# Loading the first x tile in one piece, splitting the rest of W1, and an uneven last chunk, in a kernel that TensorE bounds

## The chip, the cores and the metric

The kernel runs on one core of a Trainium2 chip. The metric is device time in microseconds (us) of that core. All runs compared here are of the state "fast". The profile shows one execution; its span (first to last instruction) is 1.3 to 1.4 us shorter than the device time of the same execution.

TensorE is "PE" in the profile (its weight loads are "PEld"), VectorE is DVE, ScalarE is ACT, GpSimd is POOL, and SP (SPq) is the engine whose queue issues most transfers. A label such as L624 is a line of the kernel that the trace belongs to; the same matmuls are L620 in the changed kernel.

## The reference

For x of 2048 rows and 640 features, all in bf16:

```python
g = sigmoid((x * gate_w).sum(-1))                 # one gate per row
Bu = x @ B_bar.T                                  # complex
h[t] = Lam_bar * h[t-1] + Bu[t]                   # a linear recurrence over the rows
a = 2 * Re(h @ C.T) + x * Dskip
b = gelu(x @ w1 + b1) @ w2 + b2                   # 640 -> 1728 -> 640
out = g * a + (1 - g) * b
```

The front of the program, which the change is about, is the first product `x @ w1` for the first 512 rows. It needs x with features on partitions (xT), and W1.

## The kernel before

The front loads W1 in five slabs of 128 features. For slabs 0 and 1 of x, a plain load brings rows onto partitions and TensorE transposes them; slabs 2 to 4 come by a DMA transpose. The rest of W1's columns (1024 to 1727) is one load. Here are the parts that matter, with cuts marked by `...`:

```python
xnat(0, 0)                                   # x slab 0: 128 x 4 x 128, pieces of 256 B
for h in range(2):                           # W1 slab 0, two halves, pieces of 1024 B
    load(f"w1_0{h}", "sp", ...)
xnat(1, 1.2)                                 # x slab 1, pieces of 256 B
w1load(1, "sp", 1.3)                         # W1 slab 1, pieces of 2048 B
w1load(2, "sp", 2)
xtrans(0, range(KN, KD), 3, 1.8)             # x slabs 2 to 4 by DMA transpose
w1load(3, "sp", 4)
w1load(4, "sp", 5)
load("w1_r", "sp", "l_w1r", W1sb[:, :, FW:F], ...)          # rest of W1, pieces of 1408 B
# then the DMA transposes of B
...
# five small parameter rows, issued on ScalarE's queue; the last is the tail of b1
load("b1b", "act", "l_b1b", rows[RT:RT + 1, :]..., ["b1b"], prio=-96, dur=0.4)
...
for n in (512, 512, 512, 512, 512, 256):     # TensorE warms up on constants
    t = nc.tensor.matmul(PS[5][:, 0:n], one.broadcast_to([128, 128]), ...)
...                                          # per slab: 4 transposes, one copy of 128 x 512; then a fill matmul
op("cols", "pe", 0.3, list(ROWS) + ["b1b", "ident"], [("bank", 7)], f_cols, prio=9.5)   # rows -> columns
...
seq = [(k, jf) for k in range(KD) for jf in range(NW)]      # 40 matmuls: 5 slabs x 8 banks
...
# end: the last chunk's output in two halves of 320 columns, each combined and stored on its own
```

A small list scheduler orders each engine's work when the program is built. "cols" turns the parameter rows into columns with one transpose on TensorE, between the ninth and the tenth of the 40 matmuls.

Of the kernel before, what the change touches and what calls it, by code (L numbers as in the profile page):

```python
# [184 lines left out]
def bass_gated_mix__ssm_conv_s5__dense_activation_gelu__prompt_kernel(  # L185
# [40 lines left out]
    with ExitStack() as es:  # L226
# [76 lines left out]
        def inc(eng, ins):  # L303
            return E.inc(eng, ins, eng + "_s")
# [46 lines left out]

        KN = 2

        def xnat(k, prio):
            load(f"xna{k}", "sp", f"l_xna{k}", xn[0][:, :, k * 128:(k + 1) * 128],
                 x2[0:512, k * 128:(k + 1) * 128].rearrange("(c p) d -> p c d", p=128), [("xna", k)], prio, dur=0.45, lat=2.0)

        xnat(0, 0)
        for h in range(2):
            fs = slice(h * FW // 2, (h + 1) * FW // 2)  # L360
            load(f"w1_0{h}", "sp", f"l_w10{h}", W1sb[:, 0, fs], B_w1[0:128, fs], [("w1", 0, h)], 0.1 + h, dur=0.45, lat=2.0)
        xnat(1, 1.2)
        w1load(1, "sp", 1.3)
        w1load(2, "sp", 2)
        xtrans(0, range(KN, KD), 3, 1.8)
        w1load(3, "sp", 4)
        w1load(4, "sp", 5)
        load("w1_r", "sp", "l_w1r", W1sb[:, :, FW:F], B_w1[:, FW:F].rearrange("(k p) f -> p k f", p=128), [("w1", "r")], prio=20, lat=5.0)

        ROWS = {"lre": (0, A_Lambda_re), "lim": (KP, A_Lambda_im), "ldt": (2 * KP, A_log_dt), "b1a": (3 * KP, B_b1[0:nmain])}  # L370
        RT = 3 * KP + NF - 1
# [27 lines left out]

        def f_warm():  # L400
            t = None
            for n in (512, 512, 512, 512, 512, 256):
                t = nc.tensor.matmul(PS[5][:, 0:n], one.broadcast_to([128, 128]), one.broadcast_to([128, n]), start=True, stop=True)
            return inc("pe", t)

        op("warm", "pe", 2.5, (), [("bank", 5)], f_warm, prio=-1000)

        for k in range(KN):
            bank = 7 - k
            pt = PS[bank][:, :].bitcast(BF16)[:, 0:512]  # L410

            def f_xt(k=k, pt=pt):
                t = None
                for c in range(4):
                    t = nc.tensor.transpose(pt[:, c * 128:(c + 1) * 128], xn[0][:, c, k * 128:(k + 1) * 128], ident[:, :])
                return inc("pe", t)

            op(f"xt{k}", "pe", 0.44, [("xna", k), "ident"], [("bank", bank)], f_xt, prio=(-990, 4.5)[k])

            def f_xc(k=k, pt=pt):  # L420
                return inc("dve", nc.vector.tensor_copy(out=xT[0][:, k, :], in_=pt))

            op(f"xc{k}", "dve", 0.42, [("bank", bank)], [("xT", 0, k)], f_xc, prio=-2000 + k)

        def f_fill():
            return inc("pe", nc.tensor.matmul(PS[5][:, :], one.broadcast_to([128, 128]), one.broadcast_to([128, 512]), start=True, stop=True))

        op("fill", "pe", 0.4, (), [("bank", 5)], f_fill, prio=-980)

        XT = {q: [("xT", q, k) for k in range(KD)] for q in range(NQ)}  # L430

        psC = PS[7][:, :].bitcast(BF16)[:, 0:128]

# [135 lines left out]
        for ci, src in enumerate((A_B_re, A_B_im)):  # L569
# [1 line left out]
        xtrans(1, range(KD), 32, 3.4)  # L571
        load("gwb", "sp", "l_gwb", gwb[:, :], gate_w.partition_broadcast(128), ["gwb"], prio=32.2)
        load("xnb", "sp", "l_xnb", xn[0][:, :, KN * 128:D], x2[0:512, KN * 128:D].rearrange("(c p) d -> p c d", p=128),
             [("xn", 0, 0), ("xn", 0, 1)], 32.4, dur=1.0, lat=6.0, reads=[("xna", 0), ("xna", 1)])
        load("w2a", "sp", "l_w2a", W2sb[:, 0:NF - 1, :], B_w2[0:nmain, :].rearrange("(j p) d -> p j d", p=128), ["w2a"], prio=33, lat=8.0)
        load("w2b", "sp", "l_w2b", W2sb[0:FL, NF - 1, :], B_w2[nmain:F, :], ["w2b"], prio=34, lat=4.0)
        load("w2c", "sp", "l_w2c", W2sb[64:64 + FL, NF - 1, :], B_w2[nmain:F, :], ["w2c"], prio=34.2, lat=4.0)
# [39 lines left out]
        def m1_first():  # L617
            seq = [(k, jf) for k in range(KD) for jf in range(NW)]
            seq.remove((0, NW - 1))
            seq.insert(seq.index((1, NW - 1)), (0, NW - 1))  # L620
            for k, jf in seq:

                def f_mm(jf=jf, k=k):
                    return inc("pe", nc.tensor.matmul(PS[jf][:, :], W1sb[:, k, jf * 128:(jf + 1) * 128], xT[0][:, k, :],  # L624
                                                      start=(k == 0), stop=(k == KD - 1)))

                op(f"m1_0_{jf}_{k}", "pe", d_mm(512), [("xT", 0, k), ("w1", k) if k else ("w1", 0, jf // (NW // 2))], [("bank", jf)] ,
                   f_mm, prio=pe_prio())
            for jf in range(NW):
                ctr["bank"] += 1  # L630

                def f_ge(jf=jf):
                    return inc("act", nc.scalar.activation(Gl[0][:, jf, :], PS[jf][:, :], ACT.Gelu_apprx_tanh, bias=b1col[:, jf:jf + 1]))

                op(f"ge_0_{jf}", "act", d_act(512), [("bank", jf), "b1col"], [("gl", 0, jf)], f_ge, prio=10)

        def m1(q, j0=0):
            for jf in range(j0, NF - 1):
                bank = next_bank()

                def f_mm(jf=jf, bank=bank):
                    t = None
                    for k in range(KD):
                        t = nc.tensor.matmul(PS[bank][:, :], W1sb[:, k, jf * 128:(jf + 1) * 128], xT[q][:, k, :],  # L644
                                             start=(k == 0), stop=(k == KD - 1))
                    return inc("pe", t)

                op(f"m1_{q}_{jf}", "pe", KD * d_mm(512), XT[q] + ([("w1", 0, 0), ("w1", 0, 1)] + [("w1", k) for k in range(1, KD)] if jf < NW else [("w1", "r")]), [("bank", bank)], f_mm, prio=pe_prio())

                def f_ge(jf=jf, bank=bank):  # L650
                    return inc("act", nc.scalar.activation(Gl[q % 2][:, jf, :], PS[bank][:, :], ACT.Gelu_apprx_tanh, bias=b1col[:, jf:jf + 1]))  # L651

                op(f"ge_{q}_{jf}", "act", d_act(512), [("bank", bank), "b1col"], [("gl", q % 2, jf)], f_ge, prio=10)

        def m1_tail(q):
            bank = next_bank()

            def f_mm():
                t = None
                for k in range(KD):  # L660
                    for i in range(2):
                        t = nc.tensor.matmul(PS[bank][64 * i:64 * i + FL, :], W1sb[:, k, nmain:F], xT[q + i][:, k, :],  # L662
                                             start=(k == 0), stop=(k == KD - 1))
                return inc("pe", t)

            op(f"m1t_{q}", "pe", KD * d_mm(512) + 0.25, XT[q] + XT[q + 1] + [("w1", "r")], [("bank", bank)], f_mm, prio=pe_prio())
            for i in range(2):
                for u in range(2):

                    def f_ge(i=i, u=u):  # L670
                        return inc("act", nc.scalar.activation(Gl[i][64 * u:64 * u + FL, NF - 1, :], PS[bank][64 * i:64 * i + FL, :], ACT.Gelu_apprx_tanh,
                                                               bias=b1col[64 * i:64 * i + FL, NF - 1:NF]))

                    op(f"get_{q}_{i}{u}", "act", d_act(512), [("bank", bank), "b1col"], [("gt", i, u)], f_ge, prio=10)
# [126 lines left out]
                op(f"e1_{c}_{hf}", "act", d_act(HALF), [("bank", bank), ("g", q)], [("E1", c % NE, hf)], f_ev, prio=5)  # L801

        cbank = {}

        def cproj(c):
            q, b, s = c // 4, c // 2, c % 2
            for hf in range(2):
                bank = next_bank()
                cbank[hf] = bank
                cols = slice(hf * HALF, (hf + 1) * HALF)  # L810

                def f_mm(bank=bank, cols=cols):
                    t = None
                    i = 0
                    for ci in range(2):
                        for k in range(KP):
                            t = nc.tensor.matmul(PS[bank][:, 0:HALF], H[b % NHB][:, ci, k, s * 128:(s + 1) * 128], CT[:, ci, k, cols],  # L817
                                                 start=(i == 0), stop=(i == 2 * KP - 1))
                            i += 1
                    return inc("pe", t)  # L820

                op(f"c_{c}_{hf}", "pe", 2 * KP * d_mm(HALF), [("H", b % NHB), ("CT", 0), ("CT", 1)], [("bank", bank)], f_mm, prio=pe_prio())

                if c == NCH - 1:
                    continue
# [6 lines left out]
        def comb(c):  # L832
# [8 lines left out]
            if c == NCH - 1:  # L841
# [2 lines left out]

                op("last", "dve", d_dve(D, 2), [("xg", c % 2), ("E1", c % NE, 0), ("E1", c % NE, 1)], [("E2", c % NE, 0), ("E2", c % NE, 1)], f_half, prio=-50)
                for hf in range(2):
                    cols = slice(hf * HALF, (hf + 1) * HALF)

                    def f_fin(hf=hf, cols=cols):
                        return inc("dve", nc.vector.scalar_tensor_tensor(out=osb[c % NO][:, cols], in0=PS[cbank[hf]][:, 0:HALF], scalar=gcol[:, c:c + 1],  # L850
                                                                        in1=E2[c % NE][:, cols], op0=ALU.mult, op1=ALU.add))

                    op(f"fin{hf}", "dve", d_dve(HALF), [("bank", cbank[hf]), ("E2", c % NE, hf)], [("osb", c % NO, hf)], f_fin, prio=-60)

                    def f_st(hf=hf, cols=cols):
                        return dma_inc("sp", nc.sync.dma_start(o2[c * 128:(c + 1) * 128, cols], osb[c % NO][:, cols]), f"stl{hf}")

                    op(f"stl{hf}", "sp", 0.5, [("osb", c % NO, hf)], [], f_st, prio=1000 + c, lat=2.5)
# [115 lines left out]
```

## Time and profile before

| | before |
|---|---|
| device time, median of the first three runs | 214.8 us (214.79 to 215.0) |
| profiled span | 213.9 us |
| TensorE busy | 98% of the span |
| first of the 40 W1 matmuls | 4.32 us |
| 41st W1 matmul, the first that needs the rest of W1 | 14.54 us |
| last store landed | 213.82 us |

From the page of the kernel before: engine shares, and the chain of work that ended last.

```profile
PE 209.4 (98%) x1254; PEld 119.4 (56%) x1264; DVE 188.6 (88%) x261; ACT 113.4 (53%) x205; POOL 2.5 (1%) x10
...
PE 92%; DMA 3%; SPq 3%; issue 1%; DVE 0%
PE ps L771 26%; PE ps L644 22%; PE ps L817 21%; PE ps L684 20%; DMA W1sb<-in_B_w_dram 3%; SPq L325 2%; PE ps L785 1%; PE ps L662 1%; SPq L332 1%; DVE osb L850 0%
```

TensorE is the bound, and what is not TensorE in the chain is, apart from the last combine of 0.55 us, the issuing queue and one load of W1, all before 14.54 us. The timeline of TensorE alone in the kernel before shows it (start, duration, line, what; in brackets the idle time before it and what ended it):

```profile
4.32 1.04 PE L624 MATMUL ps<-xT,W1sb 128*128 128x512 bf16 x4 [0.15 <-DVE xT L421]
5.19 0.39 PE L415 MATMUL ps<-ident,xn 128*128 128x128 bf16 x4
5.41 1.07 PE L624 MATMUL ps<-xT,W1sb 128*128 128x512 bf16 x3
6.72 0.60 PE L624 MATMUL ps<-xT,W1sb 128*128 128x512 bf16 x2 [0.24 <-DMA W1sb<-in_B_w_dram]
7.17 0.22 PE L435 MATMUL ps<-ident,rows 128*128 128x128 bf16 x1
7.22 7.03 PE L624 MATMUL ps<-xT,W1sb 128*128 128x512 bf16 x30
14.54 5.57 PE L644 MATMUL ps<-xT,W1sb 128*128 128x512 bf16 x25 [0.28 <-DMA W1sb<-in_B_w_dram]
```

At full clock the starts of neighbouring matmuls are 0.216 us apart. A matmul's recorded duration (0.379 us for 512 columns) is longer, so the records overlap, and lost time is read from the starts. By starts, TensorE lost 0.25 us at 6.10 (PSUM bank not yet copied out), 0.41 us at 6.72 (W1 slab 1), 0.17 us at 8.90 (transposed x), and 0.45 us at 14.54 (rest of W1). The waits of the weight loads name the same releasers (engine, line, releaser: us in total, times, longest):

```profile
PEld ps L624 <- DVE xT L421: 1.3, 2, 0.7
PEld ps L644 <- DMA W1sb<-in_B_w_dram: 0.8, 1, 0.8
PEld ps L624 <- DMA W1sb<-in_B_w_dram: 0.5, 1, 0.5
PEld ps L624 <- DMA xT<-in_A_x_dram: 0.5, 1, 0.5
```

The tail of the kernel before, from the timeline: the last 20 matmuls, the last combine, the two last stores.

```profile
208.73 2.88 PE L817 MATMUL ps<-CT,H 128*128 128x320 bf16 x20
...
210.87 1.69 SPq L856 DMA_DIRECT2D out_dram<-osb  x2
211.65 0.55 DVE L850 SCALAR_TENSOR_TENSOR osb<-ps,gcol,E 128x320 bf16<-128x320 f32 x1 [0.81 <-PE ps L817]
```

### The profile page before, as it was taken

To read this page: it belongs to the slowest core of one execution; us is meant where nothing else is said; L and a number is where in the kernel's file an instruction comes from. 1 tells how busy PE (TensorE), PEld (TensorE's weight loads), DVE (VectorE), ACT (ScalarE), POOL (GpSimd) and SP (SyncE) were. 2 spreads that over 40 slices of the span, in tenths; PEclk is the share of its full clock that TensorE was granted. 3 is DMA by queue.
4 is the path that set the end of the run, shared out by engine and by line. 5 is a ranking of instruction groups with operands and counts; after the bars stand their busy time and mean duration, and the time that the engine had idled before them with its cause. 6 is when DMAs were issued, how large, how long until landed. Compare 5 with 4: busy or idle time off the path is not lost.

```text
span 213.9 us, 3103 instructions
## 1 busy us (share of the span) xinstructions
PE 209.4 (98%) x1254; PEld 119.4 (56%) x1264; DVE 188.6 (88%) x261; ACT 113.4 (53%) x205; POOL 2.5 (1%) x10
## 2 busy tenths in 40 slices
PE   8999999999999999999999999999999999999995
PEld 3334444444567675444467767444446777677673
DVE  1699999999799999999999959999999998989712
ACT  2478556679544234557835332556786554535230
POOL 1000000000000010000000010000000000000000
DMA  6999899999001040000000023000000010001001
GB/s 145 287 226 213 159 357 259 215 216 168 0 0 34 31 123 34 31 0 0 0 3 0 31 45 144 13 18 0 3 0 2 0 34 31 31 3 61 31 34 31
DMA packets 30986, 16.08 MB, mean 75 GB/s; under 512 B 23932, under 2 KB 30204, under 8 KB 30972
## 3 DMA queue, kind: packets, MB, share of 16 engines
q1 hardware_dynamic: 30624, 14.57, 28.8%
q0 software_dynamic: 288, 1.31, 2.0%
q8 instruction: 10, 0.16, 0.3%
q14 instruction: 4, 0.03, 0.0%
q10 hardware_dynamic: 60, 0.01, 0.0%
HBM read 7.63 MB, written 2.62 MB: 48 GB/s over the span
## 4 chain that ended last, share of the span: by engine, by line
PE 92%; DMA 3%; SPq 3%; issue 1%; DVE 0%
PE ps L771 26%; PE ps L644 22%; PE ps L817 21%; PE ps L684 20%; DMA W1sb<-in_B_w_dram 3%; SPq L325 2%; PE ps L785 1%; PE ps L662 1%; SPq L332 1%; DVE osb L850 0%
## 5 line engine op out<-in xcount | busy, mean ns | idle before, releaser
L771 PE MATMUL ps<-W2sb,Gl 128*128 128x320 bf16 x416 | 59.1, 299 | 0.0
L771 PEld LDWEIGHTS ps<-W2sb,Gl 128*128 128x128 bf16 x416 | 40.6, 98 | 16.5 <-ACT Gl L651 0.4
L644 PE MATMUL ps<-xT,W1sb 128*128 128x512 bf16 x215 | 47.6, 379 | 0.5 <-DMA W1sb<-in_B_w_dram 0.3
L817 PE MATMUL ps<-CT,H 128*128 128x320 bf16 x320 | 46.2, 299 | 0.0
L724 DVE TENSOR_TENSOR_SCAN W<-atab,V 128x1280 bf16<-128x1280 f32 x16 | 44.3, 2811 | 0.3
L684 PE MATMUL ps<-xT,BT 128*128 128x512 bf16 x196 | 43.1, 379 | 0.3 <-issue 0.2
L817 PEld LDWEIGHTS ps<-CT,H 128*128 128x128 bf16 x320 | 30.7, 98 | 13.5 <-issue 1.6
L799 ACT ACTIVATE E<-ps,g1col 128x320 bf16<-128x320 f32 x32 | 16.1, 526 | 40.5 <-PE ps L785 21.5
L644 PEld LDWEIGHTS ps<-xT,W1sb 128*128 128x128 bf16 x220 | 21.5, 98 | 26.5 <-DMA W1sb<-in_B_w_dram 0.8
L651 ACT ACTIVATE Gl<-ps,cols 128x512 bf16<-128x512 f32 x44 | 29.8, 690 | 11.9 <-PE ps L644 11.9
L684 PEld LDWEIGHTS ps<-xT,BT 128*128 128x128 bf16 x200 | 19.5, 98 | 23.5 <-ACT Gl L651 0.4
L693 ACT ACTIVATE U<-ps 128x512 bf16<-128x512 f32 x40 | 23.6, 595 | 15.7 <-PE ps L684 15.7
L828 ACT ACTIVATE E<-ps,gcol 128x320 bf16<-128x320 f32 x30 | 15.8, 528 | 17.9 <-PE ps L817 17.9
L758 ACT ACTIVATE ps<-b2b 128x320 f32<-128x320 bf16 x32 | 14.1, 441 | 1.0
L836 DVE SCALAR_TENSOR_TENSOR xg<-xn,gcol,dsk 128x640 bf16<-128x640 bf16 x16 | 13.8, 882 | 0.4
L485 DVE TENSOR_TENSOR osb<-xg,E 128x640 bf16<-128x640 bf16 x15 | 7.3, 486 | 7.7 <-ACT E L828 7.6
L601 DVE SCALAR_TENSOR_TENSOR scr<-xn,gwb 128x640 bf16<-128x640 bf16 x16 | 13.2, 823 | 0.4
L485 DVE TENSOR_TENSOR V<-V,W 128x1280 bf16<-128x1280 bf16 x16 | 12.5, 822 | 0.3
L485 DVE TENSOR_TENSOR H<-H,V 128x1280 bf16<-128x1280 bf16 x16 | 12.5, 821 | 0.3
L485 DVE TENSOR_TENSOR V<-mr,U 128x2560 bf16<-128x2560 bf16 x8 | 11.9, 1490 | 0.2
L485 DVE TENSOR_TENSOR H<-c,W 128x2560 bf16<-128x2560 bf16 x8 | 11.9, 1488 | 0.1
L485 DVE TENSOR_TENSOR V<-s,W 128x2560 bf16<-128x2560 bf16 x8 | 11.9, 1484 | 0.0
(81 smaller groups left out, 102.5 us busy)
## 6 DMA issues: line engine op xcount, KB each, us to landing
out_dram<-osb SPq DMA_DIRECT2D x15, 160.0 KB, 1.8
W2sb<-in_B_w_dram SPq DMA_DIRECT2D x1, 2080.0 KB, 11.6
xn<-in_A_x_dram POOLq DMA_DIRECT2D x2, 640.0 KB, 4.9
W1sb<-in_B_w_dram SPq DMA_DIRECT2D x4, 256.0 KB, 3.6
W1sb<-in_B_w_dram SPq DMA_DIRECT2D x1, 880.0 KB, 7.1
xn<-in_A_x_dram SPq DMA_DIRECT2D x1, 640.0 KB, 6.1
xn<-in_A_x_dram SPq DMA_DIRECT2D x1, 384.0 KB, 6.0
xn<-in_A_x_dram SPq DMA_DIRECT2D x2, 128.0 KB, 2.5
```

What stands on the lines that cost most here:

```text
L485: return inc("dve", nc.vector.tensor_tensor(out=o, in0=a, in1=b, op=o_))
L644: t = nc.tensor.matmul(PS[bank][:, :], W1sb[:, k, jf * 128:(jf + 1) * 128], xT[q][:, k, :], start=(k == 0), stop=(k == KD - 1))
L651: return inc("act", nc.scalar.activation(Gl[q % 2][:, jf, :], PS[bank][:, :], ACT.Gelu_apprx_tanh, bias=b1col[:, jf:jf + 1]))
L684: t = nc.tensor.matmul(PS[bank][:, :], BT[:, ci, kd, k * 128:(k + 1) * 128], xT[q][:, kd, :], start=(kd == 0), stop=(kd == KD - 1))
L693: return inc("act", nc.scalar.activation(dst, src, ACT.Copy, scale=1.0 if ci == 0 else -1.0))
L724: t = inc("dve", nc.vector.tensor_tensor_scan(out=g[:, ci, :], data0=a, data1=v[:, ci, :], initial=0.0, op0=ALU.mult, op1=ALU.add))
L758: return inc("act", nc.scalar.activation(PS[bank][:, 0:HALF], b2b[:, cols], ACT.Copy))
L771: t = nc.tensor.matmul(PS[bank][:, 0:HALF], Gl[q % 2][:, jf, t4 * 128:(t4 + 1) * 128], W2sb[:, jf, cols], start=False, stop=False, skip_gr ...
L799: return inc("act", nc.scalar.activation(E1[c % NE][:, cols], PS[bank][:, 0:HALF], ACT.Copy, scale=g1col[:, c:c + 1]))
L817: t = nc.tensor.matmul(PS[bank][:, 0:HALF], H[b % NHB][:, ci, k, s * 128:(s + 1) * 128], CT[:, ci, k, cols], start=(i == 0), stop=(i == 2 ...
L828: return inc("act", nc.scalar.activation(E2[c % NE][:, cols], PS[bank][:, 0:HALF], ACT.Copy, scale=gcol[:, c:c + 1]))
L836: return inc("dve", nc.vector.scalar_tensor_tensor(out=xg[c % 2][:, :], in0=xn[q % 2][:, c % 4, :], scalar=gcol[:, c:c + 1], in1=dsk[:, :] ...
```

## The change

The intent: let slabs 0 and 1 of x come in one load with pieces of 512 B, so the transfer queue spends less time; transpose both slabs before the first W1 matmul, so that the stream has no insertions (the warm-up gets one more matmul of 512 columns, and the fill matmul goes); let the rest of W1 come in two loads, so that the 41st matmul waits for half; and make the last piece of work smaller. The diff, cut:

```diff
-        xnat(0, 0)
+        load("xna", "sp", "l_xna", xn[0][:, :, 0:KN * 128], x2[0:512, 0:KN * 128]..., ["xna"], 0, ...)
         for h in range(2): ...                       # W1 slab 0
-        xnat(1, 1.2)
         w1load(1, "sp", 1.3)
 ...
-        load("w1_r", "sp", "l_w1r", W1sb[:, :, FW:F], ..., [("w1", "r")], prio=20, lat=5.0)
+        FM = FW + 3 * 128
+        for i, (f0, f1) in enumerate(((FW, FM), (FM, F))):
+            load(f"w1_r{i}", "sp", f"l_w1r{i}", W1sb[:, :, f0:f1], ..., [("w1", "r", i)], prio=20 + i, lat=5.0)
 ...
-            for n in (512, 512, 512, 512, 512, 256):
-                t = nc.tensor.matmul(PS[5][:, 0:n], ...)
+            for n in (512,) * 6 + (256,):
+                t = nc.tensor.matmul(PS[4][:, 0:n], ...)
 ...
-        for k in range(KN):                          # 4 transposes and one copy per slab
+        for i, (k, c0, c1) in enumerate(((0, 0, 2), (0, 2, 4), (1, 0, 4))):   # slab 0 in two copies, then slab 1
 ...
-        op("fill", "pe", 0.4, (), [("bank", 5)], f_fill, prio=-980)
 ...
+        CCOLS = (slice(0, D - 256), slice(D - 256, D))        # last chunk: 384 and 256 columns
```

More of the change, by code (lines that the diff above doesn't have):

```diff
@@ L352, in bass_gated_mix__ssm_conv_s5__dense_activation_gelu__prompt_kernel @@
         KN = 2
-        def xnat(k, prio):
-            load(f"xna{k}", "sp", f"l_xna{k}", xn[0][:, :, k * 128:(k + 1) * 128],
-                 x2[0:512, k * 128:(k + 1) * 128].rearrange("(c p) d -> p c d", p=128), [("xna", k)], prio, dur=0.45, lat=2.0)
-        xnat(0, 0)
+        load("xna", "sp", "l_xna", xn[0][:, :, 0:KN * 128], x2[0:512, 0:KN * 128].rearrange("(c p) d -> p c d", p=128), ["xna"], 0, dur=0.45, lat=2.0)
         for h in range(2):
@@ L367, in bass_gated_mix__ssm_conv_s5__dense_activation_gelu__prompt_kernel @@
         w1load(4, "sp", 5)
-        load("w1_r", "sp", "l_w1r", W1sb[:, :, FW:F], B_w1[:, FW:F].rearrange("(k p) f -> p k f", p=128), [("w1", "r")], prio=20, lat=5.0)
+        FM = FW + 3 * 128
+        for i, (f0, f1) in enumerate(((FW, FM), (FM, F))):
+            load(f"w1_r{i}", "sp", f"l_w1r{i}", W1sb[:, :, f0:f1], B_w1[:, f0:f1].rearrange("(k p) f -> p k f", p=128), [("w1", "r", i)], prio=20 + i, lat=5.0)
         ROWS = {"lre": (0, A_Lambda_re), "lim": (KP, A_Lambda_im), "ldt": (2 * KP, A_log_dt), "b1a": (3 * KP, B_b1[0:nmain])}
@@ L401, in f_warm @@
             t = None
-            for n in (512, 512, 512, 512, 512, 256):
-                t = nc.tensor.matmul(PS[5][:, 0:n], one.broadcast_to([128, 128]), one.broadcast_to([128, n]), start=True, stop=True)
+            for n in (512,) * 6 + (256,):
+                t = nc.tensor.matmul(PS[4][:, 0:n], one.broadcast_to([128, 128]), one.broadcast_to([128, n]), start=True, stop=True)
             return inc("pe", t)
-        op("warm", "pe", 2.5, (), [("bank", 5)], f_warm, prio=-1000)
-        for k in range(KN):
-            bank = 7 - k
-            pt = PS[bank][:, :].bitcast(BF16)[:, 0:512]
-            def f_xt(k=k, pt=pt):
+        op("warm", "pe", 2.7, (), [("bank", 4)], f_warm, prio=-1000)
@@ L413, in f_xt @@
+        for i, (k, c0, c1) in enumerate(((0, 0, 2), (0, 2, 4), (1, 0, 4))):
+            bank = 7 - i
+            pt = PS[bank][:, :].bitcast(BF16)[:, 0:(c1 - c0) * 128]
+            def f_xt(k=k, pt=pt, c0=c0, c1=c1):
                 t = None
-                for c in range(4):
-                    t = nc.tensor.transpose(pt[:, c * 128:(c + 1) * 128], xn[0][:, c, k * 128:(k + 1) * 128], ident[:, :])
+                for c in range(c0, c1):
+                    t = nc.tensor.transpose(pt[:, (c - c0) * 128:(c - c0 + 1) * 128], xn[0][:, c, k * 128:(k + 1) * 128], ident[:, :])
@@ L416, in f_xt @@
                 return inc("pe", t)
-            op(f"xt{k}", "pe", 0.44, [("xna", k), "ident"], [("bank", bank)], f_xt, prio=(-990, 4.5)[k])
-            def f_xc(k=k, pt=pt):
-                return inc("dve", nc.vector.tensor_copy(out=xT[0][:, k, :], in_=pt))
-            op(f"xc{k}", "dve", 0.42, [("bank", bank)], [("xT", 0, k)], f_xc, prio=-2000 + k)
-        def f_fill():
-            return inc("pe", nc.tensor.matmul(PS[5][:, :], one.broadcast_to([128, 128]), one.broadcast_to([128, 512]), start=True, stop=True))
@@ L428, in bass_gated_mix__ssm_conv_s5__dense_activation_gelu__prompt_kernel, with f_xc @@
-        op("fill", "pe", 0.4, (), [("bank", 5)], f_fill, prio=-980)
-        XT = {q: [("xT", q, k) for k in range(KD)] for q in range(NQ)}
+            op(f"xt{i}", "pe", 0.11 * (c1 - c0), ["xna", "ident"], [("bank", bank)], f_xt, prio=-990 + i)
+            def f_xc(k=k, pt=pt, c0=c0, c1=c1):
+                return inc("dve", nc.vector.tensor_copy(out=xT[0][:, k, c0 * 128:c1 * 128], in_=pt))
+            op(f"xc{i}", "dve", 0.42, [("bank", bank)], [("xT", 0, k, c0)], f_xc, prio=-2000 + i)
+        XK0 = [[("xT", 0, k)] for k in range(KD)]
@@ L432, in bass_gated_mix__ssm_conv_s5__dense_activation_gelu__prompt_kernel @@
+        XK0[0] = [("xT", 0, 0, 0), ("xT", 0, 0, 2)]
+        XK0[1] = [("xT", 0, 1, 0)]
+        XT = {q: [("xT", q, k) for k in range(KD)] for q in range(1, NQ)}
+        XT[0] = [t for x in XK0 for t in x]
         psC = PS[7][:, :].bitcast(BF16)[:, 0:128]
@@ L573, in bass_gated_mix__ssm_conv_s5__dense_activation_gelu__prompt_kernel @@
         load("xnb", "sp", "l_xnb", xn[0][:, :, KN * 128:D], x2[0:512, KN * 128:D].rearrange("(c p) d -> p c d", p=128),
-             [("xn", 0, 0), ("xn", 0, 1)], 32.4, dur=1.0, lat=6.0, reads=[("xna", 0), ("xna", 1)])
+             [("xn", 0, 0), ("xn", 0, 1)], 32.4, dur=1.0, lat=6.0, reads=["xna"])
         load("w2a", "sp", "l_w2a", W2sb[:, 0:NF - 1, :], B_w2[0:nmain, :].rearrange("(j p) d -> p j d", p=128), ["w2a"], prio=33, lat=8.0)
@@ L625, in f_mm @@
                                                       start=(k == 0), stop=(k == KD - 1)))
-                op(f"m1_0_{jf}_{k}", "pe", d_mm(512), [("xT", 0, k), ("w1", k) if k else ("w1", 0, jf // (NW // 2))], [("bank", jf)] ,
+                op(f"m1_0_{jf}_{k}", "pe", d_mm(512), XK0[k] + [("w1", k) if k else ("w1", 0, jf // (NW // 2))], [("bank", jf)] ,
                    f_mm, prio=pe_prio())
@@ L646, in f_mm @@
                     return inc("pe", t)
-                op(f"m1_{q}_{jf}", "pe", KD * d_mm(512), XT[q] + ([("w1", 0, 0), ("w1", 0, 1)] + [("w1", k) for k in range(1, KD)] if jf < NW else [("w1", "r")]), [("bank", bank)], f_mm, prio=pe_prio())
+                op(f"m1_{q}_{jf}", "pe", KD * d_mm(512), XT[q] + ([("w1", 0, 0), ("w1", 0, 1)] + [("w1", k) for k in range(1, KD)] if jf < NW else [("w1", "r", int(jf * 128 >= FM))]), [("bank", bank)], f_mm, prio=pe_prio())
                 def f_ge(jf=jf, bank=bank):
@@ L664, in f_mm @@
                 return inc("pe", t)
-            op(f"m1t_{q}", "pe", KD * d_mm(512) + 0.25, XT[q] + XT[q + 1] + [("w1", "r")], [("bank", bank)], f_mm, prio=pe_prio())
+            op(f"m1t_{q}", "pe", KD * d_mm(512) + 0.25, XT[q] + XT[q + 1] + [("w1", "r", 1)], [("bank", bank)], f_mm, prio=pe_prio())
             for i in range(2):
@@ L809, in cproj, with f_mm @@
                 cbank[hf] = bank
-                cols = slice(hf * HALF, (hf + 1) * HALF)
-                def f_mm(bank=bank, cols=cols):
+                cols = CCOLS[hf] if c == NCH - 1 else slice(hf * HALF, (hf + 1) * HALF)
+                n = cols.stop - cols.start
+                def f_mm(bank=bank, cols=cols, n=n):
                     t = None
@@ L816, in f_mm @@
                         for k in range(KP):
-                            t = nc.tensor.matmul(PS[bank][:, 0:HALF], H[b % NHB][:, ci, k, s * 128:(s + 1) * 128], CT[:, ci, k, cols],
+                            t = nc.tensor.matmul(PS[bank][:, 0:n], H[b % NHB][:, ci, k, s * 128:(s + 1) * 128], CT[:, ci, k, cols],
                                                  start=(i == 0), stop=(i == 2 * KP - 1))
@@ L820, in f_mm @@
                     return inc("pe", t)
-                op(f"c_{c}_{hf}", "pe", 2 * KP * d_mm(HALF), [("H", b % NHB), ("CT", 0), ("CT", 1)], [("bank", bank)], f_mm, prio=pe_prio())
+                op(f"c_{c}_{hf}", "pe", 2 * KP * d_mm(n), [("H", b % NHB), ("CT", 0), ("CT", 1)], [("bank", bank)], f_mm, prio=pe_prio())
                 if c == NCH - 1:
@@ L846, in comb @@
                 for hf in range(2):
-                    cols = slice(hf * HALF, (hf + 1) * HALF)
+                    cols = CCOLS[hf]
                     def f_fin(hf=hf, cols=cols):
-                        return inc("dve", nc.vector.scalar_tensor_tensor(out=osb[c % NO][:, cols], in0=PS[cbank[hf]][:, 0:HALF], scalar=gcol[:, c:c + 1],
+                        return inc("dve", nc.vector.scalar_tensor_tensor(out=osb[c % NO][:, cols], in0=PS[cbank[hf]][:, 0:cols.stop - cols.start], scalar=gcol[:, c:c + 1],
                                                                         in1=E2[c % NE][:, cols], op0=ALU.mult, op1=ALU.add))
-                    op(f"fin{hf}", "dve", d_dve(HALF), [("bank", cbank[hf]), ("E2", c % NE, hf)], [("osb", c % NO, hf)], f_fin, prio=-60)
+                    op(f"fin{hf}", "dve", d_dve(HALF), [("bank", cbank[hf]), ("E2", c % NE, 0), ("E2", c % NE, 1)], [("osb", c % NO, hf)], f_fin, prio=-60)
                     def f_st(hf=hf, cols=cols):
```

## The prediction

> **What bounds it now.** TensorE. The busy table has PE at 98% of a 213.9 us span; the chain of waits is PE for 92%. From 14.54 us on, the timeline's matmuls follow each other without a hole (0.216 us start to start for 512 columns, 0.136 for 320) to the last C matmul at about 211.4; then a fixed tail: combine 0.55 us, a store landing at 213.8. Only the stretch before 14.54 us and the tail can give time. The front holds 40 matmuls (8.6 us), so "faster by 2%" (4.3 us) is out of reach.
>
> **Where the front loses time** (starts of single matmuls, landings of each load's 16 parts):
> - first W1 matmul at 4.32 us (x slab 0 landed 3.14, transposes, copy 0.42);
> - 0.25 us: seventh bank waits for the second slab's copy;
> - 0.41 us: W1 slab 1 landed 6.68;
> - 0.17 us: DMA-transposed x landed 8.85;
> - 0.45 us: rest of W1 landed 14.49, PE free at 14.09.
> The DMA share is near full from 2 to 12 us: one saturated ring.
>
> **What the change does.**
> 1. x: 64 packets of 256 B per engine become 32 of 512 B. A 256 B packet takes 17 ns, a 1024 B one 46 at best; I estimate 27 for 512 B, so the ring gains about 0.2 us. The Trainium skill ("DMA: Bandwidth & Descriptors", Specifications) puts line rate at 512 B and more; the trace agrees in direction: 15 GB/s per engine at 256 B, 24 at 2048 B.
> 2. The combined load lands about 0.3 us later than slab 0 (3.45). The longer warm-up (one more cold matmul, 0.427 us) ends at 3.5, hiding it. Four cold transposes (0.107 us each), two half copies: first W1 matmul at about 4.55, 0.2 us later. Absorbed: seven matmuls end at about 6.05, W1 slab 1 lands about 6.4. The clock should be warm by then as now ("TensorE: Matmul & The Clock Gate", Part 1: 427 ns cold, 216 warm; the trace shows both).
> 3. Bank wait, inserted transposes and fill vanish, but into the wait for W1 slab 1: no gain of their own.
> 4. Binding is the landing of the DMA-transposed x, about 8.6 instead of 8.85; then 24 matmuls, 5.18 us: PE free at 13.85.
> 5. Rest of W1: the first load (480 KB of 880) lands about 12-12.8, free of the stragglers of the single load (parts landed 12.67 to 14.49) and of the B transpose queued behind. The 0.45 us wait disappears. The second is needed 3.2 us later. B_re landed 18.0; needed about 19.25.
> 6. End: the last half shrinks from 320 to 256 columns: combine -0.07 us (about 1.05 ns per column), store -0.03. Matmul work unchanged.
>
> Sum: 0.45 + 0.2 + 0.1 = about 0.8 us, all on the critical path, since PE has no hole later. VectorE keeps slack: second H block ends 72.24, used from 73.85; last 199.98, used from 202.47.
>
> **Predicted: 214.0 us, 8 in 10 between 213.3 and 214.6.** Faster by over 2%: 0.01; within: 0.97; slower: 0.02.
>
> **What would show it.** Right: x landing near 3.45; first W1 matmul 4.5-4.6; still a wait for W1 slab 1; none for the W1 rest; later PE pieces 0.6-0.9 us earlier; last combine about 0.48 us. Wrong: a hole before the B products (B_re late), a wait at 73 or 202 us for H.
>
> **What would make it wrong.** Straggling packets: single reads of W1 took up to 0.8 us and a transpose waits for the slowest engine, so x's landing could move +-0.4 us. A cold clock at the first matmuls (0.2 us each). The list scheduler may reorder VectorE or ScalarE work and eat the slack.

## The result

The changed kernel took 214.49 us (median of 4 runs, 214.32 to 214.86) beside 214.8 us (median of 4, 214.53 to 215.0). Its ratio to the kernel before is 0.9989, with a 95% interval of 0.9971 to 1.0006: the class "same", and inside the predicted range of 213.3 to 214.6. A ratio here is the mean time of one kernel's fast runs over that of the other's fast runs of the same rounds, so not quite the ratio of the medians. The kernel was timed twice more, among the experiments: 0.9983 (0.9968 to 0.9997) and 0.9974 (0.9958 to 0.9989). The gain is thus 0.24, 0.37 and 0.56 us of about 214.9, where 0.8 us was forecast.

The profiled span fell from 213.9 to 213.1 us, which looks like the forecast 0.8 us exactly. It is one execution against one, and a main point of what follows is that this agreement is partly luck. From the page after, the lines that answer to those above:

```profile
PE 210.2 (99%) x1264; PEld 119.9 (56%) x1264; DVE 188.7 (89%) x262; ACT 113.2 (53%) x205; POOL 2.5 (1%) x10
...
PE 99%; DVE 0%; issue 0%
```

The chain is now TensorE from the warm-up on. The timeline of TensorE in the changed kernel:

```profile
3.71 1.03 PE L412 MATMUL ps<-ident,xn 128*128 128x128 bf16 x8
4.70 2.49 PE L620 MATMUL ps<-xT,W1sb 128*128 128x512 bf16 x9
7.15 0.22 PE L431 MATMUL ps<-ident,rows 128*128 128x128 bf16 x1
7.20 6.85 PE L620 MATMUL ps<-xT,W1sb 128*128 128x512 bf16 x31
13.89 5.56 PE L640 MATMUL ps<-xT,W1sb 128*128 128x512 bf16 x25
```

All four waits of before are gone: no bracket names a transfer. The 41st matmul starts at 13.89 instead of 14.54 us. But nine matmuls before the parameter transpose took 2.49 us, although nine at full clock, counted with the last one's duration, take 8 x 0.216 + 0.379 = 2.1 us. The starts show why: the first two are 0.40 and 0.41 us apart, the cold clock. And the parameter transpose started 0.12 us after TensorE could have begun it; the last small row, of the five small loads that it needs, had landed at 7.01 us, 0.13 us before. (The same distance shows in a later trace, all_again, where the profile names that row as what ended the wait.) The waits of the weight loads in the changed kernel agree, with no transfer of W1 or x among them ("issue" is a wait that the profile ascribes to nothing):

```profile
PEld ps L620 <- issue: 0.5, 2, 0.3
PEld ps L431 <- issue: 0.4, 1, 0.4
PEld ps L620 <- DVE xT L418: 0.2, 1, 0.2
```

The tail of the changed kernel:

```profile
208.07 2.88 PE L815 MATMUL ps<-CT,H 128*128 128x384 bf16 x20
...
210.54 1.29 SPq L854 DMA_DIRECT2D out_dram<-osb  x2
210.99 0.48 DVE L848 SCALAR_TENSOR_TENSOR osb<-ps,gcol,E 128x256 bf16<-128x256 f32 x1 [0.47 <-PE ps L815]
```

The last combine takes 0.48 instead of 0.55 us. Between the front and the tail nothing changed: from the 41st W1 matmul to the start of the last C matmul it is 196.77 us before and 196.79 us after. (The 0.02 us belongs to the end: of the last chunk's two halves, the first now has the 384 columns.)

### The profile page after: what moved, and what is told of

Same layout as the page of the kernel before. It is cut to its first block, busy times and chain, and to the rows that moved or that the text cites. A ratio compares the mean times of both kernels' runs of the same rounds, so it can differ in the third digit from the quotient of the medians.

```text
span 213.1 us, 3114 instructions
## 1 busy us (share of the span) xinstructions
PE 210.2 (99%) x1264; PEld 119.9 (56%) x1264; DVE 188.7 (89%) x262; ACT 113.2 (53%) x205; POOL 2.5 (1%) x10
## 3 DMA queue, kind: packets, MB, share of 16 engines
q1 hardware_dynamic: 30752, 14.57, 27.2%
## 4 chain that ended last, share of the span: by engine, by line
PE 99%; DVE 0%; issue 0%
PE ps L767 27%; PE ps L640 22%; PE ps L815 21%; PE ps L680 20%; PE ps L620 4%; PE ps L400 1%; PE ps L781 1%; PE ps L658 1%; PE ps L412 0%; DVE osb L848 0%; PE ps L431 0%
## 5 line engine op out<-in xcount | busy, mean ns | idle before, releaser
L640 PE MATMUL ps<-xT,W1sb 128*128 128x512 bf16 x220 | 48.1, 379 | 0.0
L815 PE MATMUL ps<-CT,H 128*128 128x320 bf16 (+2 forms) x320 | 46.1, 299 | 0.0
L680 PE MATMUL ps<-xT,BT 128*128 128x512 bf16 x200 | 43.8, 379 | 0.0
```

What stands on the lines that cost most here:

```text
L640: t = nc.tensor.matmul(PS[bank][:, :], W1sb[:, k, jf * 128:(jf + 1) * 128], xT[q][:, k, :], start=(k == 0), stop=(k == KD - 1))
L680: t = nc.tensor.matmul(PS[bank][:, :], BT[:, ci, kd, k * 128:(k + 1) * 128], xT[q][:, kd, :], start=(kd == 0), stop=(kd == KD - 1))
L815: t = nc.tensor.matmul(PS[bank][:, 0:n], H[b % NHB][:, ci, k, s * 128:(s + 1) * 128], CT[:, ci, k, cols], start=(i == 0), stop=(i == 2 * K ...
```

## The experiments

Twelve kernels ran, in three calls of four, each with five rounds beside the kernel before. Each call had another chip, so ratios are compared across calls, not medians. All gave correct results. Landings are times at which the last part of a load counted its semaphore, as the trace has them. The theory after the result was: the three parts act separately, the W1 split removes the wait for the rest of W1, and the x part meets two costs that the prediction lacked, a cold clock and a late parameter row. Rivals: the x part alone is the gain; the wait for the rest of W1 was one unlucky execution; the removed fill matmul made the clock cold.

### Which part does what

**Only the x part** (changed kernel with these edits undone):

```diff
-        for i, (f0, f1) in enumerate(((FW, FM), (FM, F))):
-            load(f"w1_r{i}", ...)
+        load("w1_r", "sp", "l_w1r", W1sb[:, :, FW:F], ..., [("w1", "r")], prio=20, lat=5.0)
-        CCOLS = (slice(0, D - 256), slice(D - 256, D))
+        CCOLS = (slice(0, HALF), slice(HALF, D))
```

> The x part alone (one 512 B load, eight transposes at once, longer warm-up); rest of W1 in one load, last chunk 320/320. Theory A (parts complement each other: the front removes the earlier holes, but the single W1 rest still lands at about 14.2 to 14.5 us behind the stragglers and the B transpose): PE is free at about 13.9 us and waits 0.3 to 0.6 us for the W1 rest; span within 0.2 us of before. Rival (the front alone is the gain): no wait for the W1 rest, PE goes on at about 13.9 us, span 0.5 to 0.7 us shorter.

Measured: 214.76 us, ratio 0.9990 (0.9978 to 1.0002), span 213.5. My theory of the wait failed and the rival's held: the single load of the rest landed at 12.38 us, and TensorE took the 41st matmul without a wait for it. The rival's numbers were missed, though: 14.22 us instead of about 13.9, and a span 0.3 us shorter in place of 0.5 to 0.7. Its TensorE timeline:

```profile
4.80 2.54 PE L618 MATMUL ps<-xT,W1sb 128*128 128x512 bf16 x9
7.48 0.22 PE L429 MATMUL ps<-ident,rows 128*128 128x128 bf16 x1
7.53 6.85 PE L618 MATMUL ps<-xT,W1sb 128*128 128x512 bf16 x30
14.22 5.56 PE L638 MATMUL ps<-xT,W1sb 128*128 128x512 bf16 x25
```

The stream is as closed as in the changed kernel. (30 records instead of 31 are one missing record, not a missing matmul.) What it lost lies before 7.5 us: 0.43 us to the cold clock, 0.30 us to the last small row, which landed at 7.34 us.

**Only the split of the rest of W1** (kernel before with the two loads):

```diff
-        load("w1_r", "sp", "l_w1r", W1sb[:, :, FW:F], ..., [("w1", "r")], prio=20, lat=5.0)
+        for i, (f0, f1) in enumerate(((FW, FM), (FM, F))):
+            load(f"w1_r{i}", ...)
```

> The split of the W1 rest alone. Theory A: the 0.45 us wait for the W1 rest vanishes, the matmuls after the first 40 begin at about 14.1 us instead of 14.5, span 0.3 to 0.45 us shorter. Rival (the wait in the trace of before was one unlucky execution): the time is the same within 0.1 us.

Measured: 214.84 us, ratio 0.9993 (0.9981 to 1.0005), span 213.5. The mechanism held: the first of the two loads landed at 12.22 us, the wait is gone, and the 41st matmul starts at 14.18 us, as was expected:

```profile
7.30 7.04 PE L626 MATMUL ps<-xT,W1sb 128*128 128x512 bf16 x30
14.18 5.56 PE L646 MATMUL ps<-xT,W1sb 128*128 128x512 bf16 x25
```

The time moved by 0.15 us with an interval that holds zero, so the time alone would not have shown it.

**Only the uneven end** (kernel before with 384 and 256 columns in the last chunk):

```diff
-                cols = slice(hf * HALF, (hf + 1) * HALF)
+                cols = CCOLS[hf] if c == NCH - 1 else slice(hf * HALF, (hf + 1) * HALF)
```

> The 384/256 split of the last chunk alone. Theory: from the last matmul's end to the last landing 0.1 us shorter (combine 0.48 instead of 0.55 us); time 0.05 to 0.15 us shorter, hardly told from noise. Rival: it changes nothing, because the last store's landing does not depend on 512 against 640 B rows, gain 0.05 us or less.

Measured: 215.0 us, ratio 1.0001 (0.9986 to 1.0015). The time shows nothing. The trace shows the tail plainly: from the start of the last C matmul to the last landing it is 2.35 us here and in all three traces of the changed kernel, and 2.51 to 2.53 us in the five traces with even halves (two of the kernel before, two of the x part alone, one of the W1 split alone). That is 0.16 us, of which the combine is 0.07. But counted from the 41st W1 matmul, the last C matmul starts about 0.02 us later, as the first half is now the larger one. From the 41st W1 matmul to the last landing it is 199.13 to 199.15 us with the uneven end and 199.27 to 199.29 with even halves, so the end is worth 0.14 us. The timeline of the tail:

```profile
208.67 2.88 PE L819 MATMUL ps<-CT,H 128*128 128x384 bf16 x20
...
211.14 1.29 SPq L858 DMA_DIRECT2D out_dram<-osb  x2
211.59 0.48 DVE L852 SCALAR_TENSOR_TENSOR osb<-ps,gcol,E 128x256 bf16<-128x256 f32 x1 [0.47 <-PE ps L819]
```

This trace also served the clock question. Its front is that of the kernel before, fill matmul included, and yet its first four W1 matmuls are cold:

```profile
4.25 1.89 PE L624 MATMUL ps<-xT,W1sb 128*128 128x512 bf16 x4
```

**The changed kernel again**, no edit:

> The changed kernel once more, for its spread and a second trace. If the 0.8 us between the two profiled spans is what the change is worth, the ratio is 0.9963 or near it; if the first traces were a slow execution of the one and a fast one of the other, it is 0.998 to 0.999. The first W1 matmuls are again at the cold spacing (0.40 us) if the removed fill matmul is what keeps the clock cold; if the clock's window merely fell differently, they are at 0.216 us in some traces.

Measured: 214.78 us, ratio 0.9983 (0.9968 to 0.9997), span 213.5. The first pair of traces had indeed flattered the change: its execution of the kernel before took 215.18 us, 0.38 us above that kernel's median, and its execution of the changed kernel 214.48 us, at the median. Here the clock was warm almost at once (0.09 us lost), but TensorE then waited 0.26 us for W1 slab 1 (landed 6.63 us) and 0.48 us for the small row (landed 7.47 us); the 41st matmul started at 14.35 us. This time the profile names the releaser:

```profile
4.81 2.47 PE L620 MATMUL ps<-xT,W1sb 128*128 128x512 bf16 x9
7.60 0.22 PE L431 MATMUL ps<-ident,rows 128*128 128x128 bf16 x1 [0.32 <-DMA rows<-in_B_b_dram]
```

### Is the wait for the rest of W1 real, and what is the noise?

**The kernel before against itself**, no edit:

> The kernel before, against itself: the ratio should be 1.000 within 0.0012; this is the noise. Its trace is a second sample: if the wait for the rest of W1 (0.45 us) is a property of the kernel, it shows again at 0.3 to 0.5 us; if stragglers are chance, it may be absent.

Measured: 215.06 us, ratio 0.9999 (0.9980 to 1.0018). So effects under about 0.4 us are at the edge of what five rounds can tell, and I lean on traces for them. The wait is a property of this kernel: 0.54 us here, after 0.45 and 0.18 us in the other two traces with the same front and a single load (the kernel before and the uneven end alone). From its view of waits:

```profile
PEld ps L624 <- DMA W1sb<-in_B_w_dram: 0.9, 2, 0.5
PEld ps L644 <- DMA W1sb<-in_B_w_dram: 0.9, 1, 0.9
PEld ps L624 <- DMA xT<-in_A_x_dram: 0.6, 1, 0.6
```

**The x part alone, again**, same kernel as only_x:

> The x part alone, second sample: does the single W1 rest wait or not? In its first trace the load had landed whole at 12.4 us and TensorE did not wait; in three traces of the front of before it landed at 14.4 to 14.7 and TensorE waited 0.2 to 0.5 us. If that was chance, this trace has a landing after 14 us; if it belongs to the new front, it lands at about 12.4 us again and the split of the W1 rest is worth nothing beside the x part.

Measured: 214.79 us, ratio 0.9993 (0.9978 to 1.0007). The single load landed at 13.31 us, which is neither of the two times that I had named, and was not waited for; the 41st matmul started at 14.00 us:

```profile
7.30 6.85 PE L618 MATMUL ps<-xT,W1sb 128*128 128x512 bf16 x30
14.00 2.32 PE L638 MATMUL ps<-xT,W1sb 128*128 128x512 bf16 x10
```

In two of two traces, then, the x part alone already removes the wait that the W1 split was made for, and in one trace the W1 split alone removes it too. The two parts of the change largely buy the same 0.2 to 0.5 us: the 41st matmul starts at 14.11 us with the x part alone (mean of two traces) and at 14.07 us with both (mean of three). Why the single load lands earlier behind the new front (12.4 and 13.3 us against 14.4 to 14.7) stays open in part. Its first read starts 0.2 to 0.6 us earlier (9.42 and 9.14 us against 9.59 to 9.70). And behind the old front 95% of its reads had ended by 12.8 to 13.1 us, while a last string of reads, about 60 ns apart, ran on to 14.0 to 14.2 us. That looks like one DMA engine behind the others; what put it behind is not shown. That the split is an insurance against such a late load is not shown either: behind the new front no load of the rest of W1, whole or second half, landed after 13.73 us, before the 41st matmul of its trace.

### The late small row

**Parameter transpose later** (changed kernel, after the 12th W1 matmul):

```diff
-        op("cols", "pe", 0.3, list(ROWS) + ["b1b", "ident"], [("bank", 7)], f_cols, prio=9.5)
+        op("cols", "pe", 0.3, list(ROWS) + ["b1b", "ident"], [("bank", 7)], f_cols, prio=12.5)
```

> The changed kernel with the parameter transpose (rows to columns) moved from after the 9th W1 matmul to after the 12th on TensorE. Theory (the changed kernel meets a new wait: the last small parameter row lands at 7.0 to 7.5 us, and TensorE stands at its transpose for 0.1 to 0.5 us): no hole before that transpose, the 41st W1 matmul starts 0.1 to 0.4 us earlier relative to the first one than in the two traces of the changed kernel (9.19 and 9.53 us), ratio to before 0.0005 to 0.002 lower than that of the changed kernel. Rival (the DMA-transposed x binds anyway, landing at 8.4 to 8.8 us): the hole reappears there and the time is the same. It also reorders a few VectorE items later, which could only cost if TensorE waits for H.

Measured: 214.61 us, ratio 0.9979 (0.9960 to 0.9998). The hole before the transpose is gone although the row landed at 7.54 us, and the clock was warm from the first matmul. But TensorE then waited for the transfers in its place: 0.12 us for the second half of W1 slab 0 (5.78), 0.26 us for W1 slab 1 (6.69) and 0.13 us for the transposed x (8.86). From first to 41st matmul it took 9.27 us, between the 9.19 and 9.53 of the two earlier traces. The theory of the hole held, but its gain of 0.1 to 0.4 us between first and 41st matmul is not shown; the rival was right that the next transfer takes over. On TensorE's timeline the transpose now follows the twelfth matmul, with no bracket of its own:

```profile
4.82 3.17 PE L620 MATMUL ps<-xT,W1sb 128*128 128x512 bf16 x12 [0.22 <-DVE xT L418]
7.83 0.22 PE L431 MATMUL ps<-ident,rows 128*128 128x128 bf16 x1
```

The build-time scheduler also swapped some later VectorE items; TensorE had no hole there.

**The tail of b1 first on ScalarE's queue**:

```diff
-             ..., ["b1b"], prio=-96, dur=0.4)
+             ..., ["b1b"], prio=-101, dur=0.4)
```

> The changed kernel with the last small row (tail of b1) issued first of the five small loads on ScalarE's queue. Theory (it is late because it is last in that queue, while its engine's reads stall at 3.5 to 4.5 us): it lands before 4 us; but the row before it becomes last and lands at 5 to 6 us, so no wait at the parameter transpose (needed at about 6.9 us). Rival (any last load of that queue lands at about 7 us): the wait stays as it was.

Measured: 214.8 us, ratio 0.9988 (0.9970 to 1.0006). The rival won. The moved row landed at 3.57 us, but the load that is now last landed at 7.10 us, and TensorE lost 0.69 us at the transpose. Without a fill matmul, the clock was warm from the first matmul (nine take 2.15 us):

```profile
4.70 2.15 PE L620 MATMUL ps<-xT,W1sb 128*128 128x512 bf16 x9 [0.24 <-DVE xT L418]
7.37 0.22 PE L431 MATMUL ps<-ident,rows 128*128 128x128 bf16 x1 [0.52 <-DMA rows<-in_B_b_dram]
```

So it is not that row: in these traces it is whichever of the five small loads is last in that queue.

**The tail of b1 on GpSimd's queue**, with the orders on TensorE and VectorE unchanged:

```diff
-        load("b1b", "act", "l_b1b", ...
+        load("b1b", "pool", "l_b1b", ...
-             ..., ["b1b"], prio=-96, dur=0.4)
+             ..., ["b1b"], prio=-50, dur=0.4)
```

> The changed kernel with one edit: the last small row (tail of b1) is issued on GpSimd's queue; orders on TensorE and VectorE are the same as in the changed kernel. Theory (the wait of 0.1 to 0.7 us at the parameter transpose comes from the fifth load of ScalarE's queue, which lands at 7.0 to 7.5 us): the four others land by about 5.3, the transpose follows the ninth W1 matmul without a hole; the 41st matmul at 13.7 to 14.0 us, limited by the DMA-transposed x (8.4 to 8.8, plus 5.23). Rival (the small rows are late because the engines stall, whichever queue they are on): the fourth or the moved row lands at about 7 us and the hole stays.

Measured: 214.62 us, ratio 0.9978 (0.9959 to 0.9998), span 213.5. The theory's first half held: the moved row landed at 4.25 us, the other four by 5.05, and no hole remains. But this execution's clock was cold for the first four matmuls (0.82 us lost), and the 41st matmul came at 14.34 us, outside what I had expected:

```profile
4.81 2.94 PE L620 MATMUL ps<-xT,W1sb 128*128 128x512 bf16 x9
7.59 0.22 PE L431 MATMUL ps<-ident,rows 128*128 128x128 bf16 x1
```

In this trace no transfer is waited for after the first matmul, and the clock alone costs as much as the holes of the other traces. It does not show a front without transfers to wait for: W1 slab 1 landed at 6.70 us and the transposed x at 8.86, so a warm clock would have met them.

### Transfers at the head

**Two loads of 256 B pieces at the head** (as cols_later, but x in two loads, and the short warm-up):

```diff
-        load("xna", "sp", "l_xna", xn[0][:, :, 0:KN * 128], ...)
+        for k in range(KN):
+            load(f"xna{k}", "sp", f"l_xna{k}", xn[0][:, :, k * 128:(k + 1) * 128], ...)
```

> As cols_later, but the two feature slabs of x in two loads of 256 B pieces, one right after the other at the head of the queue, and the warm-up as long as before. Theory (512 B pieces save ring time, but the ring does not bind; what binds is the time of the first W1 matmul): slab 0 lands at 3.1 us, first W1 matmul at 4.3 instead of 4.7 to 4.8 us, the 41st up to 0.4 us earlier unless W1 slab 1 (6.5 us) or the DMA-transposed x (8.6 us or later) binds. Rival (the ring binds): the DMA-transposed x lands 0.2 us later than in the changed kernel and the 41st matmul starts no earlier.

Measured: 214.92 us, ratio 0.9994 (0.9972 to 1.0015). Inconclusive, by my own making: slab 0 landed at 3.01 us as expected, but the scheduler put all eight transposes before the first W1 matmul, so that it waited for slab 1 (4.07) and started at 4.58 us, not 4.3. The first four matmuls were cold. The transposed x landed at 8.78 us, within the spread of the changed kernel's three traces (8.20 to 8.81) and no later than in cols_later with its 512 B pieces (8.86), so the rival's claim is not shown either. Nor is there, in this nearest pair, an earlier landing from the longer pieces. Its transfers ran at 270 and 331 GB/s in the two halves of 3.5 to 4.5 us, where cols_later has 78 and 76; they were slower before that.

**Tail of b1 on GpSimd's queue, and W1 slab 0 in one load**:

```diff
-        for h in range(2):
-            load(f"w1_0{h}", ...)                # two halves, pieces of 1024 B
+        load("w1_0", "sp", "l_w10", W1sb[:, 0, 0:FW], B_w1[0:128, 0:FW], ...)     # pieces of 2048 B
```

> As b1b_pool, and W1 slab 0 in one load of 2048 B pieces instead of two loads of 1024 B. Theory (the stall of reads at 3.5 to 4.5 us, in every trace with the combined x load, comes with the second half-row load): W1 slab 1 lands about 0.5 us earlier (5.7 to 6.0), the DMA-transposed x about 8.1, the 41st matmul at 13.4 to 13.7 us. Rival (the stall belongs to the first reads of W1, in whatever pieces): the landings stay where they are, and the first W1 matmul may even wait for slab 0.

Measured: 214.31 us, ratio 0.9974 (0.9959 to 0.9990). W1 slab 1 landed at 6.20 us and the transposed x at 8.30 us, and the 41st matmul started at 14.05 us, so the theory's numbers were all missed. Whether the landings moved at all is not shown: they are 0.50 and 0.56 us earlier than in b1b_pool (6.70 and 8.86), one trace against one, and within the changed kernel's 5.85 to 6.63 and 8.20 to 8.81. Between 3.5 and 4.5 us the transfers did run faster than in the changed kernel (229 and 186 GB/s in the two halves of that stretch, where its three traces have 68 to 140). It is as fast as the changed kernel, not faster.

**The changed kernel a third time**:

> The changed kernel a third time, beside the others of this call. Theory: ratio 0.998 to 0.9985; a hole before the parameter transpose again (0.1 to 0.5 us), 41st matmul at 13.9 to 14.35 us.

Measured: 214.45 us, ratio 0.9974 (0.9958 to 0.9989), below what I had expected. The small row landed at 6.81 us and was not waited for, because three cold matmuls (0.57 us lost) had made TensorE late:

```profile
4.70 2.68 PE L620 MATMUL ps<-xT,W1sb 128*128 128x512 bf16 x9
7.21 0.22 PE L431 MATMUL ps<-ident,rows 128*128 128x128 bf16 x1
13.96 2.32 PE L640 MATMUL ps<-xT,W1sb 128*128 128x512 bf16 x10
```

### All traces side by side

Seven of the fourteen traces, times in us; of the others, those on which a reading rests are given above. "First" and "41st" are starts of W1 matmuls. "Cold" is the time lost to wide spacing at the first matmuls, "holes" the time lost to waits between first and 41st. The x column is for the transposed x.

| trace | first | W1 slab 1 landed | x landed | last small row landed | cold | holes | 41st |
|---|---|---|---|---|---|---|---|
| before | 4.32 | 6.68 | 8.85 | 5.71 | 0 | 1.28 | 14.54 |
| before_again | 4.28 | 6.49 | 8.72 | 4.87 | 0 | 1.47 | 14.70 |
| only_end (same front) | 4.25 | 6.75 | 8.90 | 4.81 | 0.82 | 0.43 | 14.48 |
| changed | 4.70 | 6.19 | 8.40 | 7.01 | 0.38 | 0.12 | 13.89 |
| all_again | 4.81 | 6.63 | 8.81 | 7.47 | 0.09 | 0.74 | 14.35 |
| all_third | 4.70 | 5.85 | 8.20 | 6.81 | 0.57 | 0 | 13.96 |
| b1b_pool | 4.81 | 6.70 | 8.86 | 5.05 | 0.82 | 0.02 | 14.34 |

The 41st matmul moved from 14.57 us (mean of the first three) to 14.07 us (mean of the three of the changed kernel): 0.5 us. Cold clock and holes stand in for each other: where the clock is cold TensorE comes late to its operands and finds them there; where it is warm it waits.

**The clock.** Nine traces hold a record of when the granted clock rose to full and when it fell after the end: for instance 3.85 and 215.48 us in before_again, 5.49 and 213.70 in the changed kernel, 6.52 and 214.73 in b1b_pool. In every one of the nine the two are 208.21 or 211.63 us apart, which is 61 or 62 times 3.413 us. So the clock changes on a fixed beat of 3.413 us whose phase differs from execution to execution. The Trainium skill says just this ("TensorE: Matmul & The Clock Gate", Part 1): the window is 3413 ns and free-running, and does not reset when a kernel starts. The W1 matmuls that start before the rise are the cold ones: none where the rise came at 3.85 us, two at 5.49, three at 5.87 (all_third), four at 6.05 (only_end) and at 6.52. So the phase of the beat explains why the same program has none to four cold matmuls. That the removed fill matmul caused it is not borne out: only_end has the fill and four cold ones, b1b_first and cols_later have no fill and none. Whether the longer run of transposes makes a late rise more likely is open; too few traces.

## Why the prediction was right or wrong

It was right on what it was asked first: same within 2%, and 214.0 with a range of 213.3 to 214.6 against 214.49. The gain of 0.8 us was too large: 0.24 us in that comparison, 0.37 and 0.56 us in the two later ones.

Point by point:

1. *Ring gain of about 0.2 us from 512 B pieces.* Right for the packet, not shown for the landing. A 512 B packet took 27 ns, as estimated, so 19 GB/s per engine; a 256 B packet is recorded with 18 ns, where the prediction has 17, so 14 GB/s. The transposed x landed at 8.20 to 8.81 us (mean 8.47) against 8.72 to 8.90 (mean 8.82), but the changed front differs in more than the pieces, and the nearest pair (two_slabs and cols_later) shows no gain. The Trainium skill's rule ("DMA: Bandwidth & Descriptors", Specifications) points the right way.
2. *x lands at 3.45, first W1 matmul at about 4.55, clock warm.* Off: x landed at 3.65 to 3.77 us and the first matmul started at 4.70 to 4.81. The packets' length was right; the first ones came slowly (136 GB/s between 2.0 and 2.5 us, where the kernel before moved 199). The warm clock failed in two of three traces.
3. *Bank wait, insertions and fill vanish, into the wait for W1 slab 1.* The first half is right; the wait for W1 slab 1 showed in one of three traces.
4. *"Binding is the landing of the DMA-transposed x, about 8.6 instead of 8.85; then 24 matmuls, 5.18 us: PE free at 13.85."* **This step failed.** In none of the three traces did TensorE wait for the transposed x: it landed at 8.40, 8.81 and 8.20 us, and with 5.18 us for the 24 matmuls left it would have allowed about 13.6, 14.0 and 13.4 us (an estimate by the prediction's own sum). What binds is the later start of a closed stream: 4.70 to 4.81 us, plus 8.69 us of work (40 x 0.2158 + 0.056 for the parameter transpose), plus 0.50 to 0.84 us lost to the cold clock, to the last small row and to W1 slab 1. That the first trace gave 13.89, near the forecast 13.85, was a coincidence of other terms; the three traces gave 13.89, 14.35 and 13.96. The prediction had a cold clock among its doubts, but gave it no place in the sum, and it does not mention the landing of the small rows, which before the change landed at 4.8 to 5.7 us and were never waited for. The predicted wait lies close behind: in cols_later, with a warm clock and the small row out of the way, TensorE did wait 0.13 us for the transposed x.
5. *The wait for the rest of W1 disappears by the split.* It disappears, and the split alone does it in a trace. But the x part alone does it as well, so the 0.45 us and the 0.2 us of the sum are not two independent gains.
6. *The end: 0.1 us.* The mechanism was right and the size 0.14 us, in every trace.
7. *VectorE's slack, B_re in time.* Right: no TensorE hole after the 41st matmul; 196.77 us before and 196.79 after.

The mis-sized term is thus the front. The prediction had 0.69 us there (14.54 to 13.85); the traces show 0.5 us on average. With the tail's 0.14 that makes 0.64 us by traces, while the timed runs say 0.24 to 0.56. Most of the difference is in which executions were profiled: the two of the kernel before (215.18 and 215.33 us) were slower than their medians (214.8 and 215.06) by 0.38 and 0.27 us, while the three of the changed kernel lie within 0.06 us of theirs. So the traces flatter the change, and the timed runs say what it is worth.

No version beat the changed kernel beyond the noise: the row on GpSimd's queue has 0.9978, and with W1 slab 0 in one load 0.9974, beside 0.9974 for the changed kernel.

## What to carry to other kernels

When a change closes the visible waits at the head of a kernel, cost the head anew as "start of the stream + work + what is late next", and check the landing of every operand, also of tiny ones that had slack before. Before adding up the gains of several parts, ask whether two of them remove the same wait. And where effects are a few tenths of a microsecond, look at several traces: one pair of spans gave 0.8 us here and the timed runs 0.24 to 0.56.

## What the Trainium skill lacked or had wrong

- "TensorE: Matmul & The Clock Gate", Part 1, gives the rise of the clock, in its opening observation, as around 4 us into activity, varying by 500 ns. Here, with the first matmul at 0.78 us, the rise came, in the nine traces that record it, between 3.85 and 6.52 us, so 3.1 to 5.7 us into activity: a spread of 2.7 us, most of the 3.413 us window.
- "DMA: Bandwidth & Descriptors", Specifications, gives 512 B as the least size for line rate. Here there is no step at 512 B: single packets, by their most frequent recorded duration, ran at 14 GB/s per engine at 256 B (18 ns), 19 at 512 B (27 ns), 22 at 1024 B (46 ns) and 24 at 2048 B (84 ns).
- I found on no page that the last of five small loads on ScalarE's queue may land 7 us after the start while large loads run on the other queue: it landed at 6.8 to 7.5 us behind the combined x load, at 4.8 to 5.7 us behind the old front, and with one load taken off that queue the last landed at 5.05 and 6.01 us.
- I found on no page the stall of reads near the head of the program: with the combined x load the transfers of the changed kernel ran at 68 to 140 GB/s between 3.5 and 4.5 us, with single 1024 B reads of up to 1.2 us, where they run at 286 to 316 GB/s in the 0.5 us before. Its cause stays open; one load instead of two half-row loads for W1 slab 0 raised the rate there (229 and 186), and so did x in two loads (270 and 331), but that a later landing gained by it is not shown.
